# Chunked attention and a gated mixture of experts on one core: row scatters and first gathers paced by the blocks, and another order at the start

## The chip, the core and the metric

The kernel runs on one core of a Trainium2 chip. The metric is device time in microseconds (us): the median of three timed executions. A separate execution was taken with the hardware profiler; its page and its trace are what the sections below quote. Engines are named as the profile names them: PE is TensorE (PEld its weight loads), DVE VectorE, ACT ScalarE, POOL GpSimd, SP SyncE, which issues most loads.

## The reference, cut to what matters

Attention over chunks of 32 queries, each seeing 8 memory rows and a band of keys (16 to the left, 8 to the right of its chunk), feeds a mixture of 8 experts. Each token goes to one expert: a fresh argmax where a local gate is below one half, otherwise the expert of the token before it.

```python
# attention: batch 4, heads 8, seq 768, head_dim 64, n_mem 8; chunk, left, right = 32, 16, 8
for c in range(nc):
    k_full = concat([mem_k, k[:, :, l_start:r_end]]);  v_full = concat([mem_v, v[:, :, l_start:r_end]])
    scores = q_c @ k_full.T / sqrt(D)
    a = exp(scores - max);  a = a / (sum(a) + 1e-9)
    out[:, :, c_start:c_end] = a @ v_full
# bridge: (B, H, S, D) -> (B, S, H*D): x has 3072 tokens of 512

# experts: E = 8, F = 1024; w1 is (8, 512, 1024), w2 is (8, 1024, 512), all float32
logits = x @ w_gate;  local_gate = sigmoid(x @ w_local)
for b in range(B):
    prev_e = -1
    for s in range(S):
        fresh_e = argmax(logits[b, s])
        e = fresh_e if (s == 0 or local_gate[b, s] < 0.5) else prev_e
        prev_e = e
        p = softmax(logits[b, s])
        out[b, s] = p[e] * (relu(x[b, s] @ w1[e]) @ w2[e])
```

## The kernel before

The work is cut into 32 blocks of 96 tokens (NB = 32; 8 blocks a batch, NQB = 8; a half batch is HALF = 4 blocks). For each block the kernel computes transposed scores, exponentials and values, turns the block's output for the gate, and after each half batch computes logits, picks, ranks and a destination row for every token. Each block's 96 rows of x (512 values, a probability and a token number) are then scattered by an indirect DMA from the POOL queue into x_dram, where the rows of one expert stand together. Tiles of 128 rows are later gathered from there and run through one expert. The matmuls and transposes keep the program's order.

A block's work, two instructions per head in scores and one in values:

```python
def scores(qt, kt, qb):                      # 16 small matmuls with tile_position, 3 exponentials on ACT
    ...
def values(pt, vt, n, x):
    for u in range(2):
        o_ps = ops.tile([QB, HP, VW], F32, name="o_ps", tag=f"o_ps{u}")
        for a in range(HP):
            nc.tensor.matmul(o_ps[:, a], lhsT=pt[:, u, a], rhs=vt[:, 2 * a + u], start=True, stop=True)
        rinv = rinvs[:, n, u]
        nc.vector.reciprocal(rinv, o_ps[:, :, DH:VW])
        nc.vector.tensor_tensor(x[...][:, u], o_ps[:, :, 0:DH], rinv.to_broadcast([QB, HP, DH]), op=ALU.mult)

def turned(x, xt):                           # four transposes into xt_ps, then a copy on ACT
    ...
    nc.scalar.copy(xt, xt_ps)
```

The scatters of a half batch, four at once, at the end of its routing:

```python
def route_rows(r, b, half, x):
    ...
    row = sm.tile([QB, HALF], I32, name="row", bufs=2)
    nc.vector.tensor_reduce(row, r_ps, axis=AX.X, op=ALU.max)
    ...
    for n in range(HALF):
        ins = nc.gpsimd.indirect_dma_start(
            out=x_dram[:, :], out_offset=bass.IndirectOffsetOnAxis(ap=row[:, n:n + 1], axis=0),
            in_=x[0:QB, j + n].bitcast(I32), in_offset=None).ins
        ...
        scatters[b].append(ins)
```

When each step of routing runs: half batch g is routed from n = 4 g + 6 on; `first` runs ahead of a block's values, `after` behind them.

```python
for g in range(NB // HALF):
    b, half = divmod(g, 2)
    n = HALF * g + HALF + 2
    plan_at(first, n, half_logits, g)                      # lt_ps
    ...                                                    # turned logits, picks, experts, ranks: n .. n + 3
    plan_at(after, n + (4 if g in (2 * FORE - 1, 2 * B - 2, 2 * B - 1) else 5), rows, b, half)
...
n = NQB * FORE + HALF + 2                                  # 22
plan_at(after, n, plan_begun)                              # tiles of the first two batches
plan_at(after, n + 1, planned)                             # from here weights of the first two tiles
plan_at(after, n + 2, early_gathered)                      # all five early gathers
plan_at(after, NB - 3, first_turned)                       # needs the first of them
for n in range(NB - 8, NB):
    plan_at(after, n, some_pieces, 1)                      # a sixteenth of two tiles' weights each
```

The main loop and the loads ahead of it (LOADS = 4 buffers, PAIR = 2):

```python
qks = {n: load_qk(n, nc.scalar) for n in range(2)}
vts = {n: load_v(n) for n in range(LOADS - 2)}
...
begun = {n: begin(n) for n in range(PAIR)}                 # load_qk(n + 2), then scores(n)
nc.sync.dma_start(wg[:, :, 0:E], w_gate.rearrange("(k p) e -> p k e", p=P))
nc.sync.dma_start(wg[:, :, E:E + 1], w_local.rearrange("(k p) e -> p k e", p=P))
for n in range(NB):
    b, j = divmod(n, NQB)
    if n % PAIR == 0:
        for f in first.pop(n, ()):
            f()
        for m in range(n + PAIR, min(n + 2 * PAIR, NB)):
            begun[m] = begin(m)
    ...
    values(begun.pop(n), vts.pop(n), n, xs[b][0:QB, j])
    if n + LOADS - 2 < NB:
        vts[n + LOADS - 2] = load_v(n + LOADS - 2)
    if n > 0:
        turn(n - 1)
    for f in after.pop(n, ()):
        f()
```

Behind the loop come the experts' tiles: weights of one expert (4 MB a tile) into three buffers, two products, and an indirect DMA of the result rows into the output. The last routing steps (half batches 6 and 7 scatter there) stand between the matmuls of the first two tiles. The indices of the result rows are made on POOL:

```python
to = hp.tile([P, 1], I32, name="to", bufs=4)
nc.gpsimd.tensor_tensor(to, xs[:, D + 1:XW].bitcast(I32), past, op=ALU.add)
```

Of the kernel before, what the change touches and what calls it, by code (L numbers as in the profile page):

```python
# [9 lines left out]
I32 = mybir.dt.int32  # L10
ACT = mybir.ActivationFunctionType
ALU = mybir.AluOpType
# [3 lines left out]
P = 128  # L16
B, H, S, DH, NMEM = 4, 8, 768, 64, 8
CHUNK, LEFT, RIGHT = 32, 16, 8
E, F = 8, 1024
D = H * DH  # L20
DK, FK = D // P, F // P
HP = H // 2
# [5 lines left out]
QB = 96  # L28
BAND = P - NMEM
NQB = S // QB  # L30
HALF = NQB // 2
HQ = HALF * QB
NB = B * NQB
# [8 lines left out]
FORE = 2  # L42
EARLY = 5
BRANCH = SURE - 4
RING = 4
LOADS = 4
PLAN = 3 * E + 5
PAIR = 2
# [181 lines left out]
def everything(ctx, tc, q, k, v, w_gate, w_local, w1, w2, x_dram, out, ident, back):  # L230
# [4 lines left out]
    nc = tc.nc  # L235
# [29 lines left out]
    def load_v(n):  # L265
        vt = ld.tile([P, H, VW], F32, name="vt")
        nc.sync.dma_start(vt, v[n])
        return vt
# [1 line left out]

    qks = {n: load_qk(n, nc.scalar) for n in range(2)}
    qks.update({n: load_qk(n) for n in range(2, LOADS - 2)})
    vts = {n: load_v(n) for n in range(LOADS - 2)}
    table = once.tile([1, 1], F32, name="table")
    nc.scalar.activation(table, zeros[0:1, 0:1], ACT.Exp)

# [1 line left out]
    wg = once.tile([P, DK, QUARTER], F32, name="wg")  # L278
# [26 lines left out]
    for name, qb in kinds:  # L305
        lo = QB * qb - LEFT - band_start(qb) + NMEM
        hi = QB * qb + CHUNK + RIGHT - band_start(qb) + NMEM
        m = masks[name] = once.tile([P, NG], F32, name=f"mask_{name}")
# [42 lines left out]
# [4 lines that stand above are left out]
                nc.tensor.matmul(o_ps[:, a], lhsT=pt[:, u, a], rhs=vt[:, 2 * a + u], start=True, stop=True)  # L355
            rinv = rinvs[:, n, u]
            nc.vector.reciprocal(rinv, o_ps[:, :, DH:VW])
            nc.vector.tensor_tensor(  # L358
                x[:, 0:D].rearrange("p (a u d) -> p u a d", u=2, d=DH)[:, u], o_ps[:, :, 0:DH],
                rinv.to_broadcast([QB, HP, DH]), op=ALU.mult)  # L360

    def turned(x, xt):
        xt_ps = xps.tile([P, DK, QB], F32, name="xt_ps", tag="xps")
# [26 lines left out]


    scatters = {b: [] for b in range(B)}

    def begin_route():
        return {n: sm.tile([QB, NQB, w], F32, name=n, bufs=2) for n, w in (("lt", E + 1), ("ex", E))}
# [56 lines left out]
    def route_rows(r, b, half, x):  # L452

        j = HALF * half
        rank, tot, ex = r["rank"], r["tot"], r["ex"][:, j:j + HALF]
        r_ps = xps.tile([QB, HALF, E], F32, name="r_ps", tag="xps")
        for n in range(HALF):
            nc.tensor.transpose(r_ps[:, n], rank[:, QB * (j + n):QB * (j + n) + QB], identity=ident[:E, :E])
        row = sm.tile([QB, HALF], I32, name="row", bufs=2)
        nc.vector.tensor_reduce(row, r_ps, axis=AX.X, op=ALU.max)  # L460
        nc.vector.scalar_tensor_tensor(ex, r_ps, 0.0, ex, ALU.is_gt, ALU.mult)
        prob = sm.tile([QB, HALF, 1], F32, name="prob")
        nc.vector.tensor_reduce(prob, ex, axis=AX.X, op=ALU.add)
        nc.vector.tensor_tensor(x[0:QB, j:j + HALF, D:D + 1], prob, tot, op=ALU.mult)
        for n in range(HALF):
            ins = nc.gpsimd.indirect_dma_start(  # L466
                out=x_dram[:, :], out_offset=bass.IndirectOffsetOnAxis(ap=row[:, n:n + 1], axis=0),
                in_=x[0:QB, j + n].bitcast(I32), in_offset=None).ins

            tc.declare_no_dep(ins, group="scatters", query=mybir.DependencyQuery.ANY_SYNC, reason="rows are unique")  # L470
            tc.add_to_no_dep_group("scatters", ins)
            scatters[b].append(ins)

# [120 lines left out]

    SP = mybir.EngineType.SP

    def gathered(tiles, i, after, xs=None):
        _, rows, _ = tiles  # L600
        if xs is None:
            xs = gx.tile([P, XW], F32, name="xs")
        ins = nc.gpsimd.indirect_dma_start(
            out=xs.bitcast(I32), out_offset=None, in_=x_dram[:, :],
            in_offset=bass.IndirectOffsetOnAxis(ap=rows[:, i:i + 1], axis=0)).ins
        for a in after:
            for s in scatters[a]:
                tc.add_manual_dep(ins, s.name, mybir.DependencyInfo(
                    mybir.DependencyClass.Sync, mybir.DependencyReason.DATA), reason="rows written")
        tc.add_to_no_dep_group("scatters", ins)  # L610
        return xs

# [36 lines left out]
    def begin(n):  # L649
        ahead = n + LOADS - 2  # L650
        if ahead < NB:
            qks[ahead] = load_qk(ahead)
        return scores(*qks.pop(n), n % NQB)

    xs, xts, lts, routes = {}, {}, {}, {}
# [8 lines left out]
        b, half = divmod(g, 2)  # L664
        logits_turned(lts.pop(g), routes[b]["lt"][:, HALF * half:HALF * half + HALF])

    def rows(b, half):
        route_rows(routes[b], b, half, xs[b])


    first, after = {}, {}

    def plan_at(at, step, f, *args):
        at.setdefault(step, []).append(lambda: f(*args))
# [4 lines that stand above are left out]
        plan_at(first, n, half_logits, g)  # L679
        plan_at(after, n, half_turned, g)  # L680
        plan_at(after, n + 1, lambda b=b, half=half: route_picks(routes[b], half))
        plan_at(after, n + 2, lambda b=b, half=half: route_experts(routes[b], half))
        plan_at(after, n + 3, lambda b=b, half=half: route_ranks(routes[b], b, half))
        plan_at(after, n + 3, lambda b=b, half=half: route_places(routes[b], half))

        plan_at(after, n + (4 if g in (2 * FORE - 1, 2 * B - 2, 2 * B - 1) else 5), rows, b, half)

    early = {}

# [8 lines left out]
        early["w"], pieces = zip(*(weights_begun(early["tiles"], i, wa) for i in range(2)))  # L698
        early["pieces"] = [p for ps in pieces for p in ps]

    def early_gathered():
        early["xs"] = [gathered(early["tiles"], i, range(FORE)) for i in range(EARLY)]

    def rows_turned(tiles, i, xs, ps=None, xt=None):
        _, _, past = tiles
# [21 lines left out]
    n = NQB * FORE + HALF + 2  # L727
    plan_at(after, n, plan_begun)
    plan_at(after, n + 1, planned)
    plan_at(after, n + 2, early_gathered)  # L730
    plan_at(after, NB - 3, first_turned)
    for n in range(NB - 8, NB):
        plan_at(after, n, some_pieces, 1)

    begun = {n: begin(n) for n in range(PAIR)}
    nc.sync.dma_start(wg[:, :, 0:E], w_gate.rearrange("(k p) e -> p k e", p=P))
    nc.sync.dma_start(wg[:, :, E:E + 1], w_local.rearrange("(k p) e -> p k e", p=P))
    for n in range(NB):
        b, j = divmod(n, NQB)
        if n % PAIR == 0:  # L740
            for f in first.pop(n, ()):
                f()
            for m in range(n + PAIR, min(n + 2 * PAIR, NB)):
                begun[m] = begin(m)
        if j == 0:
            xs[b] = xp.tile([P, NQB, XW], F32, name="x")
            nc.gpsimd.tensor_copy(xs[b][0:QB, :, D + 1:XW].bitcast(I32), token[:, n:n + NQB])
            routes[b] = begin_route()
        if j % HALF == 0:
            xts[n // HALF] = sm.tile([P, DK, HALF, QB], F32, name="xt", bufs=2)  # L750
        values(begun.pop(n), vts.pop(n), n, xs[b][0:QB, j])
        if n + LOADS - 2 < NB:
            vts[n + LOADS - 2] = load_v(n + LOADS - 2)
        if n > 0:
            turn(n - 1)
        for f in after.pop(n, ()):
            f()
# [136 lines left out]
    for i in range(SURE):  # L894
        if i + 2 < EARLY:
            tile_w.append(weights(early["tiles"], i + 2, pools[(i + 2) % 3]))
        if i == 2:
# [3 lines left out]
            for _ in range(2):  # L901
                flat = xp.tile([P, NQB, XW], F32, name="x").rearrange("p n w -> p (n w)")
                at = 0
# [32 lines left out]
        if i + 1 < SURE:  # L936
            tiles, at_i = (early["tiles"], i + 1) if i + 1 < EARLY else (late, i + 1 - EARLY)
# [53 lines left out]
```

## Time and profile before

| | |
|---|---|
| timed, median of 3 | 498.27 us (497.16 to 498.86) |
| profiled execution | 525.75 us, span 524.0 us, mean granted clock 0.959 |
| PE busy | 493.1 us, 94% of the span |
| DVE, ACT, POOL busy | 108.8, 111.5, 98.8 us |
| moved by DMA | 146.08 MB, mean 279 GB/s |
| row scatters into x_dram | 32, 29.7 us of POOL, 927 ns each |
| first gathers | 5, 7.1 us from issue to landing |
| first lt_ps matmul | at 26.48 us |
| first expert matmul | at 137.83 us |

The page gives the busy time of each engine, then the span in 40 equal slices with the busy share in tenths, the granted clock of TensorE and the DMA share; its groups give the cost of each kind of instruction. The trace behind it answers for any stretch of time: busy time by engine, or the instructions in order with the idle time before each in brackets and what ended it.

### The profile page before, as it was taken

The page shows a single profiled execution, that of the slowest core. Times are in us where ns is not written, and L with a number is a line of the kernel's source. Part 1 is how long each engine was busy: PE and PEld are TensorE (multiplying, and loading weights), DVE is VectorE, ACT ScalarE, POOL GpSimd, SP SyncE. Part 2 cuts the span into 40 slices and gives each one's busy share as a digit, 9 for nine tenths or more (in the row PEclk, how much of TensorE's full clock was granted, in tenths as well). Part 3 has the DMA queues.
Part 4 walks back from the last instruction along what each step waited for, and adds up shares of the span by engine and source line. Part 5 has one row for each costly group of instructions (what it writes and reads, how often), then busy time and mean ns, then how long its engine had stood idle before and what let it go on. Part 6 is the DMA issues. An engine that isn't in the chain of part 4 may idle for free. (4 is left out here: it accounts for less than half of the span.)

```text
span 524.0 us, 10237 instructions
## 1 busy us (share of the span) xinstructions
PE 493.1 (94%) x3982; PEld 376.5 (72%) x3982; DVE 108.8 (21%) x437; ACT 111.5 (21%) x235; POOL 98.8 (19%) x151
## 2 busy tenths in 40 slices
PE   6998977888999999999999999999999999999993
PEld 4987865777867877777677777777767777859671
DVE  2565545643534700000100000000000000000000
ACT  4565443432211111011111111101111111101110
POOL 3002112332306212211011111111100220022201
PEclk8999778976999999999999999999999999999997
DMA  8988668699999998999899999888229999952011
GB/s 271 295 266 256 190 178 250 197 350 332 377 400 314 374 379 305 353 357 328 312 349 325 318 334 328 321 323 322 115 57 379 408 329 411 410 190 48 29 43 31
DMA packets 49381, 146.08 MB, mean 279 GB/s; under 512 B 7258, under 2 KB 11358, under 8 KB 49312
## 3 DMA queue, kind: packets, MB, share of 16 engines
q1 hardware_dynamic: 42240, 123.38, 66.2%
q0 software_dynamic: 6784, 21.30, 11.3%
q8 instruction: 38, 0.62, 0.5%
q10 hardware_dynamic: 288, 0.52, 0.3%
q14 instruction: 31, 0.25, 0.2%
HBM read 132.57 MB, written 13.00 MB: 278 GB/s over the span
## 5 line engine op out<-in xcount | busy, mean ns | idle before, releaser
L644 PE MATMUL y_ps<-w_sb,ht 128*128 128x512 f32 x224 | 98.5, 593 | 0.0
L644 PEld LDWEIGHTS h_ps<-held_xt,w_sb 128*128 128x128 f32 x704 | 80.5, 192 | 6.6 <-issue 4.9
L644 PE MATMUL h_ps<-held_xt,w_sb 128*128 128x128 f32 x704 | 81.4, 275 | 0.9 <-ACTq _compat.py:109 0.9
L644 PEld LDWEIGHTS y_ps<-w_sb,ht 128*128 128x128 f32 x224 | 41.5, 190 | 46.9 <-issue 46.2
L799 POOL DMA_INDIRECT out_dram<-y,to x24 | 24.2, 1009 | 241.9 <-ACT y L798 178.8
L644 PE MATMUL o_ps<-vt,pt 128*96 128x65 f32 x512 | 55.6, 263 | 8.2 <-DVE x L358 2.7
L644 PEld LDWEIGHTS o_ps<-vt,pt 128*96 128x96 f32 x512 | 51.4, 178 | 12.9 <-remote 2.9
L783 PEld LDWEIGHTS h_ps<-gxt,w_sb 128*128 128x128 f32 x448 | 51.2, 192 | 2.9 <-issue 2.9
L783 PE MATMUL h_ps<-gxt,w_sb 128*128 128x128 f32 x448 | 51.7, 275 | 0.0
L786 ACT ACTIVATE ht<-h_ps 128x512 f32<-128x512 f32 x42 | 25.1, 597 | 121.2 <-PE h_ps L644 76.7
L794 PE MATMUL y_ps<-w_sb,ht 128*128 128x512 f32 x112 | 49.4, 592 | 0.0
L466 POOL DMA_INDIRECT x_dram<-x,row x32 | 29.7, 927 | 93.0 <-DVE tot L448 60.6
L644 PEld LDWEIGHTS s_ps<-qt,kt 64*64 64x64 f32 x1024 | 28.7, 160 | 15.5 <-issue 11.5
L644 PE MATMUL s_ps<-qt,kt 64*64 64x96 f32 x1024 | 32.7, 283 | 6.8 <-DMA kt<-in_k_dram 3.5
L794 PEld LDWEIGHTS y_ps<-w_sb,ht 128*128 128x128 f32 x112 | 20.7, 190 | 23.0 <-issue 22.7
L711 DVE COPY held_xt<-g_ps 128x512 f32<-128x512 f32 x12 | 8.3, 689 | 137.5 <-PE g_ps L644 123.0
L644 PEld LDWEIGHTS h_ps<-x,w_sb 128*128 128x128 f32 x192 | 31.2, 190 | 1.2 <-issue 1.2
L644 PE MATMUL h_ps<-x,w_sb 128*128 128x192 f32 x192 | 31.9, 327 | 0.0
L348 ACT ACTIVATE pt<-s_ps,mask_mid 128x256 f32<-128x256 f32 x72 | 28.2, 478 | 12.3 <-PE s_ps L644 11.6
L711 DVE COPY gxt<-g_ps 128x512 f32<-128x512 f32 x10 | 6.9, 687 | 95.1 <-PE g_ps L708 52.7
L358 DVE TENSOR_TENSOR x<-o_ps,rinvs 96x256 f32<-96x256 f32 x64 | 26.2, 417 | 1.2
L798 ACT ACTIVATE y<-y_ps,x 128x512 f32<-128x512 f32 x12 | 8.2, 687 | 83.1 <-PE y_ps L644 76.4
(208 smaller groups left out, 379.3 us busy)
## 6 DMA issues: line engine op xcount, KB each, us to landing
w_sb<-in_w_dram SPq DMA_DIRECT2D x192, 512.0 KB
vt<-in_v_dram SPq DMA_DIRECT2D x32, 260.0 KB
kt<-in_k_dram SPq DMA_DIRECT2D x30, 256.0 KB
qt<-in_q_dram SPq DMA_DIRECT2D x32, 192.0 KB
kt<-in_k_dram ACTq DMA_DIRECT2D x2, 256.0 KB
x_dram<-x,row POOLq DMA_INDIRECT x32, 6.5
out_dram<-y,to POOLq DMA_INDIRECT x24, 7.5
x<-x_dram,rows_late POOLq DMA_INDIRECT x11
```

Of the source, the lines that this page charges most:

```text
L348: nc.scalar.activation(pt[:, :, :, c], st[:, :, :, c], ACT.Exp, bias=m[:, g:g + 1], scale=SCALE)
L358: nc.vector.tensor_tensor(x[:, 0:D].rearrange("p (a u d) -> p u a d", u=2, d=DH)[:, u], o_ps[:, :, 0:DH], rinv.to_broadcast([QB, HP, DH]), ...
L466: ins = nc.gpsimd.indirect_dma_start(out=x_dram[:, :], out_offset=bass.IndirectOffsetOnAxis(ap=row[:, n:n + 1], axis=0), in_=x[0:QB, j + n ...
L644: return lambda *a, **k: tc.keep_in_program_order(f(*a, **k))
L711: nc.vector.tensor_copy(xt[:, :, 0:P], g_ps)
L783: nc.tensor.matmul(h_ps[:, m], lhsT=w1_sb[:, kk, P * (g + m):P * (g + m) + P], rhs=xt[:, kk, 0:rows], start=(kk == 0), stop=(kk == DK - 1))
L786: nc.scalar.activation(ht[:, g:g + many], h_ps, ACT.Relu)
L794: nc.tensor.matmul(y_ps, lhsT=ht[:, m, 0:P], rhs=w2_sb[:, m], start=(m == 0), stop=(m == FK - 1))
L798: nc.scalar.activation(y, y_ps, ACT.Copy, scale=xs[:, D:D + 1])
L799: return apart(nc.gpsimd.indirect_dma_start(out=out, out_offset=bass.IndirectOffsetOnAxis(ap=to, axis=0), in_=y, in_offset=None, bounds_ch ...
```

## The change

Three things are moved; no arithmetic is changed, and the number of instructions on each engine stays the same but for a few waits.

- The row scatters of half batches 0, 1, 2, 4 and 5 go out one with each block: the first when the rows are known, the others behind the last VectorE multiply of the following blocks. Half batches 3, 6 and 7 still send their four at once. The five early gathers also go out one with each block, from block 24 on.
- At the start the values of block 0 come ahead of the scores of blocks 2 and 3, and block 1's v is loaded behind the q and k of blocks 2 and 3.
- The gate's weights are loaded behind the values of block 2 instead of ahead of the loop.

It is meant to keep the pipeline of TensorE, VectorE and ScalarE going while rows are scattered, and to give TensorE work while the first loads come in.

```diff
@@ -270,7 +270,7 @@
 
     qks = {n: load_qk(n, nc.scalar) for n in range(2)}
     qks.update({n: load_qk(n) for n in range(2, LOADS - 2)})
-    vts = {n: load_v(n) for n in range(LOADS - 2)}
+    vts = {0: load_v(0)}
     table = once.tile([1, 1], F32, name="table")
     nc.scalar.activation(table, zeros[0:1, 0:1], ACT.Exp)
 
@@ -355,9 +355,9 @@
                 nc.tensor.matmul(o_ps[:, a], lhsT=pt[:, u, a], rhs=vt[:, 2 * a + u], start=True, stop=True)
             rinv = rinvs[:, n, u]
             nc.vector.reciprocal(rinv, o_ps[:, :, DH:VW])
-            nc.vector.tensor_tensor(
+            paced[0] = nc.vector.tensor_tensor(
                 x[:, 0:D].rearrange("p (a u d) -> p u a d", u=2, d=DH)[:, u], o_ps[:, :, 0:DH],
-                rinv.to_broadcast([QB, HP, DH]), op=ALU.mult)
+                rinv.to_broadcast([QB, HP, DH]), op=ALU.mult).ins
 
     def turned(x, xt):
         xt_ps = xps.tile([P, DK, QB], F32, name="xt_ps", tag="xps")
@@ -390,6 +390,12 @@
 
 
     scatters = {b: [] for b in range(B)}
+
+    paced = [None]
+
+    def behind(ins, name):
+        tc.add_manual_dep(ins, name, mybir.DependencyInfo(
+            mybir.DependencyClass.Sync, mybir.DependencyReason.DATA), reason="rows written, or one a block")
 
     def begin_route():
         return {n: sm.tile([QB, NQB, w], F32, name=n, bufs=2) for n, w in (("lt", E + 1), ("ex", E))}
@@ -462,14 +468,18 @@
         prob = sm.tile([QB, HALF, 1], F32, name="prob")
         nc.vector.tensor_reduce(prob, ex, axis=AX.X, op=ALU.add)
         nc.vector.tensor_tensor(x[0:QB, j:j + HALF, D:D + 1], prob, tot, op=ALU.mult)
-        for n in range(HALF):
-            ins = nc.gpsimd.indirect_dma_start(
-                out=x_dram[:, :], out_offset=bass.IndirectOffsetOnAxis(ap=row[:, n:n + 1], axis=0),
-                in_=x[0:QB, j + n].bitcast(I32), in_offset=None).ins
-
-            tc.declare_no_dep(ins, group="scatters", query=mybir.DependencyQuery.ANY_SYNC, reason="rows are unique")
-            tc.add_to_no_dep_group("scatters", ins)
-            scatters[b].append(ins)
+        r["row"] = row
+
+    def scatter(r, b, half, n):
+        j = HALF * half + n
+        ins = nc.gpsimd.indirect_dma_start(
+            out=x_dram[:, :], out_offset=bass.IndirectOffsetOnAxis(ap=r["row"][:, n:n + 1], axis=0),
+            in_=xs[b][0:QB, j].bitcast(I32), in_offset=None).ins
+
+        tc.declare_no_dep(ins, group="scatters", query=mybir.DependencyQuery.ANY_SYNC, reason="rows are unique")
+        tc.add_to_no_dep_group("scatters", ins)
+        scatters[b].append(ins)
+        return ins
 
 
 
@@ -596,7 +606,7 @@
 
     SP = mybir.EngineType.SP
 
-    def gathered(tiles, i, after, xs=None):
+    def gathered(tiles, i, after, xs=None, then=None):
         _, rows, _ = tiles
         if xs is None:
             xs = gx.tile([P, XW], F32, name="xs")
@@ -605,8 +615,9 @@
             in_offset=bass.IndirectOffsetOnAxis(ap=rows[:, i:i + 1], axis=0)).ins
         for a in after:
             for s in scatters[a]:
-                tc.add_manual_dep(ins, s.name, mybir.DependencyInfo(
-                    mybir.DependencyClass.Sync, mybir.DependencyReason.DATA), reason="rows written")
+                behind(ins, s.name)
+        if then is not None:
+            behind(ins, then.name)
         tc.add_to_no_dep_group("scatters", ins)
         return xs
 
@@ -664,8 +675,14 @@
         b, half = divmod(g, 2)
         logits_turned(lts.pop(g), routes[b]["lt"][:, HALF * half:HALF * half + HALF])
 
-    def rows(b, half):
+    def rows(b, half, count):
+
         route_rows(routes[b], b, half, xs[b])
+        for n in range(count):
+            scatter(routes[b], b, half, n)
+
+    def moved(b, half, n):
+        behind(scatter(routes[b], b, half, n), paced[0].name)
 
 
     first, after = {}, {}
@@ -683,7 +700,13 @@
         plan_at(after, n + 3, lambda b=b, half=half: route_ranks(routes[b], b, half))
         plan_at(after, n + 3, lambda b=b, half=half: route_places(routes[b], half))
 
-        plan_at(after, n + (4 if g in (2 * FORE - 1, 2 * B - 2, 2 * B - 1) else 5), rows, b, half)
+        if g in (2 * FORE - 1, 2 * B - 2, 2 * B - 1):
+            plan_at(after, n + 4, rows, b, half, HALF)
+        else:
+            at = min(n + 5, NB - 2)
+            plan_at(after, at, rows, b, half, 1)
+            for j in range(1, HALF):
+                plan_at(after, min(at + j, NB - 1), moved, b, half, j)
 
     early = {}
 
@@ -698,8 +721,8 @@
         early["w"], pieces = zip(*(weights_begun(early["tiles"], i, wa) for i in range(2)))
         early["pieces"] = [p for ps in pieces for p in ps]
 
-    def early_gathered():
-        early["xs"] = [gathered(early["tiles"], i, range(FORE)) for i in range(EARLY)]
+    def early_gathered(i):
+        early.setdefault("xs", []).append(gathered(early["tiles"], i, range(FORE), then=paced[0]))
 
     def rows_turned(tiles, i, xs, ps=None, xt=None):
         _, _, past = tiles
@@ -727,21 +750,26 @@
     n = NQB * FORE + HALF + 2
     plan_at(after, n, plan_begun)
     plan_at(after, n + 1, planned)
-    plan_at(after, n + 2, early_gathered)
+    for i in range(EARLY):
+        plan_at(after, n + 2 + i, early_gathered, i)
     plan_at(after, NB - 3, first_turned)
     for n in range(NB - 8, NB):
         plan_at(after, n, some_pieces, 1)
 
     begun = {n: begin(n) for n in range(PAIR)}
-    nc.sync.dma_start(wg[:, :, 0:E], w_gate.rearrange("(k p) e -> p k e", p=P))
-    nc.sync.dma_start(wg[:, :, E:E + 1], w_local.rearrange("(k p) e -> p k e", p=P))
+    vts[1] = load_v(1)
+
+    def pair_begun(n):
+        for m in range(n + PAIR, min(n + 2 * PAIR, NB)):
+            begun[m] = begin(m)
+
     for n in range(NB):
         b, j = divmod(n, NQB)
         if n % PAIR == 0:
             for f in first.pop(n, ()):
                 f()
-            for m in range(n + PAIR, min(n + 2 * PAIR, NB)):
-                begun[m] = begin(m)
+            if n > 0:
+                pair_begun(n)
         if j == 0:
             xs[b] = xp.tile([P, NQB, XW], F32, name="x")
             nc.gpsimd.tensor_copy(xs[b][0:QB, :, D + 1:XW].bitcast(I32), token[:, n:n + NQB])
@@ -749,6 +777,11 @@
         if j % HALF == 0:
             xts[n // HALF] = sm.tile([P, DK, HALF, QB], F32, name="xt", bufs=2)
         values(begun.pop(n), vts.pop(n), n, xs[b][0:QB, j])
+        if n == 0:
+            pair_begun(n)
+        if n == PAIR:
+            nc.sync.dma_start(wg[:, :, 0:E], w_gate.rearrange("(k p) e -> p k e", p=P))
+            nc.sync.dma_start(wg[:, :, E:E + 1], w_local.rearrange("(k p) e -> p k e", p=P))
         if n + LOADS - 2 < NB:
             vts[n + LOADS - 2] = load_v(n + LOADS - 2)
         if n > 0:
```

## The prediction

> **What bounds the kernel now.** I read the page's slices first, then the busy time by stretches, then the order of time inside the worst stretches. The slices split the span:
>
> ```profile
> PE   6998977888999999999999999999999999999993
> ...
> PEclk8999778976999999999999999999999999999997
> DMA  8988668699999998999899999888229999952011
> ```
>
> A slice is 13.1 us. From the eleventh on (about 132 us) TensorE is full and at full clock: this is the expert stage. In the ten before it, the attention and routing, TensorE has holes and its clock falls. To size both I cut the span at the logits matmuls (lt_ps), which come once in four blocks:
>
> ```profile
> 16.48:26.48 10.00, 10.00 (x209) 9.53 (x209) 4.80 (x17) 6.51 (x16) 0.00 (x0) 1.00 0.88 284
> 26.48:38.12 11.64, 11.61 (x226) 10.44 (x225) 6.49 (x30) 7.58 (x19) 0.00 (x0) 1.00 0.85 261
> 38.12:53.83 15.71, 12.98 (x229) 11.19 (x229) 9.01 (x39) 8.10 (x20) 3.75 (x4) 0.91 0.84 261
> 53.83:72.18 18.35, 15.02 (x229) 12.86 (x229) 9.50 (x42) 7.32 (x18) 3.69 (x5) 0.78 0.67 203
> 72.18:89.12 16.94, 13.52 (x230) 11.42 (x229) 8.50 (x36) 8.09 (x20) 3.86 (x5) 0.90 0.72 219
> 89.12:106.40 17.28, 14.65 (x234) 12.41 (x234) 11.71 (x63) 7.10 (x18) 5.62 (x6) 0.92 0.62 192
> 106.40:132.08 25.68, 21.56 (x232) 18.64 (x232) 10.37 (x42) 7.98 (x20) 6.58 (x7) 0.68 0.98 341
> ...
> 140.00:518.00 378.00, 374.60 (x2161) 274.36 (x2159) 37.67 (x124) 50.99 (x86) 69.07 (x93) 1.00 0.78 288
> ```
>
> Columns: the stretch, its length, then busy time and count of PE, PEld, DVE, ACT and POOL, the granted clock, DMA share and GB/s. Four blocks without a scatter (26.48 to 38.12) take 11.64 us with TensorE full. Every later four blocks hold row scatters (POOL busy) and take 15.7 to 25.7 us for the same 229 or so matmuls. The experts are 374.6 busy of 378: nothing in this change can shorten them. What a scatter burst does shows in the order of time:
>
> ```profile
> 46.10 1.00 POOL L466 DMA_INDIRECT x_dram<-x,row  x1 [40.41 <-DVE tot L448]
> ...
> 47.40 0.92 POOL L466 DMA_INDIRECT x_dram<-x,row  x1 [0.30 <-issue]
> ...
> 47.50 0.50 PE L644 MATMUL xt_ps<-ident,x 96*128 96x96 f32 x4
> ...
> 48.18 0.18 DVE L357 RECIPROCAL rinvs<-o_ps 96x4 f32<-96x4 f32 x1 [1.67 <-PE xt_ps L644]
> ...
> 48.63 0.92 POOL L466 DMA_INDIRECT x_dram<-x,row  x1 [0.30 <-issue]
> ...
> 49.85 0.92 POOL L466 DMA_INDIRECT x_dram<-x,row  x1 [0.30 <-issue]
> ...
> 51.77 0.48 ACT L366 COPY xt<-xt_ps 128x384 f32<-128x384 f32 x1 [3.80 <-PE o_ps L644]
> ```
>
> The four transposes xt_ps end at 48.00 and ScalarE has been free since 47.96, but its copy starts at 51.77, 1.0 us after the last of four scatters has been issued (50.77). VectorE too starts late. Nothing that they wait for by name is missing; everything halts together while POOL emits row scatters, then TensorE's clock is halved.
>
> **The number that decides the size.** The profiled execution took 525.75 us, the timed ones 498.27: 27.5 us less. The experts are full in the profile, so nearly all of it must come out of the stage with the holes. Its excess over 11.64 us for four blocks is 4.07 + 6.71 + 5.30 + 5.64 + 14.04 = 35.8 us. So only about 35.8 - 27.5 = 8.3 us of excess can be left when no profile is taken. I read most of the halts as an effect of recording 96 rows for each scatter. That is an inference; no run here shows it yet. The pacing is worth a part of 8 us, not of 36.
>
> **What the Trainium skill says.** "TensorE: Matmul & The Clock Gate", section "What's actually happening": the array falls to half clock after an idle window of about 3.4 us and comes back after a busy one. The trace agrees: in 10.00 to 15.00 us, after a hole of 3.0 us in the start, the granted clock averages 0.66. "SBUF — State Buffer", section "Who interferes with whom": only VectorE and GpSimd can block each other, TensorE and ScalarE wait on no one. The trace shows ScalarE late by 3.8 us, so a port lock is not the cause. "Perfetto Trace Analysis", section on the SWDGE instruction: its slice is the making of descriptors, not the transfer. It agrees: 0.92 us slices, 6.5 us from issue to landing on the page.
>
> **The change, part by part.**
>
> *Start: values of block 0 ahead of scores 2 and 3, block 1's v behind their loads, gate weights later.* Now: scores 0 and 1 end at 6.85; scores 2 and 3 wait for kt until 9.83 and, the clock having fallen at about 10, take 2.79 us instead of 1.55; values 0 and 1 follow at 12.55; scores 4 and 5 start at 16.48. Loads ahead of them, from the page's sizes (qt 192 KB, kt 256, vt 260): four qt and kt pairs and two vt, 2312 KB = 2.37 MB by 9.83. At 321 GB/s (stretch 4.00 to 16.48, DMA share 1.00) that is 7.4 us, so the stream counts from about 2.4. After: one vt less, 0.27 MB / 321 = 0.8 us, so scores 2 and 3 start at 9.0. Values 0 (1.5 us) fill the hole at about 7.0, so I expect full clock: scores 2 and 3 end at 10.55, values 1 at 12.1, transposes at 12.4. Scores 4 and 5 need 2052 + 260 + 896 KB = 3.29 MB: 2.4 + 10.2 = 12.7. **That is 3.8 us before 16.48.** The next pair: TensorE would be ready at 12.7 + 5.0 (a pair, 16.48 to 21.48) = 17.7; the data, with three more vt and two qt, kt pairs, is 5.0 MB, 2.4 + 15.6 = 18.0, plus 0.6 for the gate's small pieces, which now stand here (from 8.50 to 9.50 DMA moved 175 GB/s where the us before moved 409: 0.57 us lost). So scores 6 and 7 start at 18.6 instead of 21.48: 2.9 us are left. Later the load stream has slack (share 0.85 to 0.88 from 16 to 38 us), so I carry 2.9, call it **3.0**.
>
> *Paced scatters.* Number of instructions unchanged: 32 scatters. Five of eight half batches (0, 1, 2, 4, 5) send one row scatter behind each block's last VectorE multiply; half batch 3 still sends four at once, because the first gathers need it, and 6 and 7 lie under the experts. Half batch 5 is cut off by the end of attention: one scatter at block 30 and three at 31, three of which POOL takes only after the result indices, which wait for the end of attention (11.5 us today). In the timed runs the five stretches keep 8.3 of 35.8 us, a factor of 0.23. The first three, whose bursts are all paced, hold 16.1, so 3.7 us timed. A single scatter still costs its 0.92 us of POOL and perhaps one short halt, so I count under half: **1.5 us**.
>
> *Paced gathers.* Five, now after blocks 22+2 to 22+6, not all at block 24. Only the first is needed before the experts (block 29). The same traffic, spread; the last stretch (106 to 132) has DMA share 0.98 with two tiles' weights. I count **0**: what is not DMA-bound there may gain, what is DMA-bound can't.
>
> Sum: 498.3 - 3.0 - 1.5 = **493.8**.
>
> **Rivals.**
> 1. *The halts are real without a profile and pacing removes them.* For it: 36 us of excess are in plain view. Against: the timed runs lack 27.5 of them. If all of the 8.3 went, with the start: 498.3 - 11.3 = 487.
> 2. *A halt comes with each scatter and is only spread.* Then the sum of halts stays, though holes under the clock's window may keep the clock up. The start alone remains: 495.3; with new holes in four times as many blocks, 499.
> 3. *DMA takes the place of the saved time.* From block 24 the loads of the last blocks, two tiles' weights (8.4 MB) and the gathers share the engines; 0.98 share, 341 GB/s. If the experts' start waits for weights, what was saved after the plan (block 23) is lost, though a saving before block 23 brings the weights forward too. Then 495 to 497.
>
> **Range and chances.** Start 2 to 4 us, pacing -2 to +6, DMA taking back 0 to 2. The eight-in-ten range is 488 to 498.5. Two per cent is 10 us, which needs rival 1 almost whole: 0.09. Slower by 10 us has no mechanism here: 0.02.
>
> **What would show it.** In the profile after: values of block 0 at about 7 us, scores 4 and 5 before 13.5, scores 6 and 7 before 19.5, no half clock at 10; if scores 4 still start after 15, the start is wrong. Stretches of four blocks between logits matmuls: nearer 12 to 14 us than 15 to 18 if pacing keeps the clock up; unchanged if halts only spread. Half batch 3's burst should still show its halt. Even a much shorter profiled span (by 15 us, say) with a timed gain of 4 to 5 would be as I expect, since the profile exaggerates the halts. The prediction is wrong if the timed gain passes 10 us (the halts were real, the 0.23 factor false), or if there is none (the start's gain was taken back by the loads).

## The result, and the profile after

The changed kernel takes 491.68 us (median of four runs, 490.64 to 492.67) against 497.72 us (four runs, 496.92 to 498.86) before: a ratio of 0.9877, interval 0.9847 to 0.9907. That is 6.0 us, where 4.5 us had been predicted. The total was near, but one step on the way to it was false, and the nearness is in part luck.

The slices of the profiled execution of the changed kernel (span 490.1 us, 12.3 us a slice) answer to those of before:

```profile
PE   8999999899999999999999999999999999999993
...
PEclk9999999999999999999999999999999999999998
...
DMA  8978999999999999988989898894179999921111
```

The holes of the first ten slices and the low clock beside them are nearly gone. The busy time by stretches, cut at the logits matmuls as before (length, then busy time and count of PE, PEld, DVE, ACT and POOL, granted clock, DMA share, GB/s):

```profile
23.09:34.73 11.64, 11.60 (x225) 10.44 (x225) 6.49 (x30) 7.59 (x19) 0.00 (x0) 1.00 0.82 264
34.73:46.71 11.98, 11.88 (x229) 10.70 (x229) 9.02 (x39) 7.65 (x20) 1.92 (x2) 1.00 0.83 261
46.71:58.63 11.92, 11.88 (x229) 10.70 (x229) 8.93 (x40) 7.53 (x20) 4.13 (x4) 1.00 0.94 292
58.63:70.61 11.98, 11.88 (x229) 10.71 (x229) 9.01 (x39) 7.65 (x20) 3.89 (x5) 1.00 0.99 316
70.61:83.95 13.34, 12.95 (x235) 11.34 (x235) 11.93 (x65) 7.53 (x19) 6.42 (x7) 1.00 0.98 310
83.95:98.94 14.99, 13.57 (x233) 12.05 (x233) 10.38 (x40) 8.07 (x20) 3.85 (x4) 0.92 1.01 364
98.94:108.87 9.93, 9.64 (x93) 8.27 (x92) 6.10 (x33) 2.12 (x5) 2.95 (x3) 0.95 1.01 404
```

Four blocks with scatters now take 11.92 to 11.98 us, with TensorE full. Even the fifth stretch, where half batch 3 still sends four at once, holds 12.95 us of PE in 13.34. It is in truth five in a row (75.39 to 80.28 us, 1.2 us apart), since the last scatter of half batch 2 falls on the same block 22. Only the sixth has a hole: TensorE waits 1.42 us for vt at 95.57 and runs at half clock from about 96.5 to 100. What follows the last logits matmul took 381 to 383 us in every recording compared here, so all differences lie ahead of it.

The profiled spans differ by 33.9 us (524.0 to 490.1), the timed runs by 6.0. The prediction read that as an effect of recording. The first experiment shows that recording alone does not bring the halts.

### The profile page after: what moved, and what is told of

Same layout as the page of the kernel before. It is cut to its first block, busy times and chain, and to the rows that moved or that the text cites. A ratio compares the mean times of both kernels' runs of the same rounds, so it can differ in the third digit from the quotient of the medians.

```text
span 490.1 us, 10242 instructions
## 1 busy us (share of the span) xinstructions
PE 476.3 (97%) x3982; PEld 364.2 (74%) x3982; DVE 109.0 (22%) x437; ACT 111.5 (23%) x235; POOL 101.1 (21%) x151
## 5 line engine op out<-in xcount | busy, mean ns | idle before, releaser
L655 PE MATMUL o_ps<-vt,pt 128*96 128x65 f32 x512 | 50.2, 251 | 1.7 <-DMA vt<-in_v_dram 1.4
L655 PEld LDWEIGHTS o_ps<-vt,pt 128*96 128x96 f32 x512 | 46.9, 166 | 5.4 <-issue 1.6
L475 POOL DMA_INDIRECT x_dram<-x,row x32 | 31.3, 978 | 63.3 <-DVE tot L454 40.8
L655 PEld LDWEIGHTS s_ps<-qt,kt 64*64 64x64 f32 x1024 | 23.0, 138 | 6.9 <-DMA qt<-in_q_dram 3.1
L734 DVE COPY gxt<-g_ps 128x512 f32<-128x512 f32 x10 | 6.9, 689 | 95.3 <-PE g_ps L731 52.8
L655 PE MATMUL s_ps<-qt,kt 64*64 64x96 f32 x1024 | 26.3, 254 | 0.9 <-DMA kt<-in_k_dram 0.9
L831 ACT ACTIVATE y<-y_ps,xs 128x512 f32<-128x512 f32 x12 | 8.3, 688 | 81.9 <-PE y_ps L827 48.3
```

The lines of the kernel that those rows point to most:

```text
L475: ins = nc.gpsimd.indirect_dma_start(out=x_dram[:, :], out_offset=bass.IndirectOffsetOnAxis(ap=r["row"][:, n:n + 1], axis=0), in_=xs[b][0: ...
L655: return lambda *a, **k: tc.keep_in_program_order(f(*a, **k))
L734: nc.vector.tensor_copy(xt[:, :, 0:P], g_ps)
L831: nc.scalar.activation(y, y_ps, ACT.Copy, scale=xs[:, D:D + 1])
```

## The experiments

All runs on one chip share the runs of the kernel before, taken beside them. Chips are called A to D in order of use; each served for one group of runs only. Ratios leave out runs more than 1.5% above the fastest of their kernel, so they differ a little from the quotient of two medians; microseconds of a gain are the ratio times the median before, unless medians are named. The stretches are four blocks each, between logits matmuls, from one recording of each kernel.

| run | chip | ratio to before | interval | first logits matmul, us | second to fourth stretch, us | fifth | sixth and seventh |
|---|---|---|---|---|---|---|---|
| before again | A | 0.9986 | 0.9959 to 1.0012 | 25.71 | 11.98, 11.92, 11.97 | 13.28 | 14.68, 16.62 |
| start only | A | 0.9948 | 0.9924 to 0.9972 | 23.31 | 11.98, 11.92, 12.13 | 13.27 | 13.65, 12.70 |
| pacing only | A | 0.9865 | 0.9816 to 0.9914 | 28.92 | 11.98, 11.92, 11.98 | 13.35 | 12.56, 9.46 |
| gathers at once | A | 0.9874 | 0.9835 to 0.9913 | 23.23 | 11.98, 11.91, 11.98 | 13.49 | 12.56, 13.58 |
| early bursts | B | 0.9831 | 0.9785 to 0.9876 | 24.32 | 16.59, 18.46, 17.77 | 18.45 | 13.86, 9.64 |
| gathers late | B | 0.9921 | 0.9899 to 0.9944 | 23.71 | 15.84, 18.99, 17.35 | 18.02 | 17.48, 10.23 |
| weights late | B | 0.9966 | 0.9942 to 0.9989 | 23.22 | 16.58, 18.69, 17.93 | 18.51 | 23.19, 10.14 |
| v ahead | B | 0.9590 | 0.9547 to 0.9632 | 23.44 | 12.53, 12.52, 12.61 | 20.97 | 14.65, 10.00 |
| changed again | C | 0.9538 | 0.9497 to 0.9579 | 25.65 | 11.98, 12.63, 12.64 | 21.13 | 14.94, 9.46 |
| all paced | C | 0.9480 | 0.9422 to 0.9538 | 24.77 | 11.98, 12.58, 12.65 | 14.56 | 14.08, 10.00 |
| plain writes | C | 0.9548 | 0.9494 to 0.9602 | 26.21 | 11.98, 12.52, 12.74 | 21.80 | 14.34, 9.46 |
| plain writes by GpSimd | D | 0.9953 | 0.9919 to 0.9988 | 22.71 | 11.99, 11.91, 19.06 | 15.03 | 12.56, 9.46 |

**The same kernel before takes 499.6 us on chip A (43 runs), 499.0 on D (20), 523.8 on B (43) and 524.6 on C (11).** The ranges do not touch: 504.9 us is the slowest on A and D, 520.3 the fastest on B and C. The timed 498 us of the comparison and the profile of 525.75 us with its halts fit these two kinds of chip. So the profile of before most likely showed a chip of the other kind than the one on which the kernel was timed. The chips of these two are not on record, nor that of the changed kernel's comparison, whose times and stretches are those of A. As no chip was used twice, it also isn't shown that a chip stays of its kind.

### Before, unchanged

No edit. 

> The kernel before, unchanged, recorded and timed again. If the halts under scatter bursts come from recording that form of program, a new profile again lies 20 us or more above the timed 497.7, with stretches of four blocks of 15 us and more. If they belonged to one recorded execution alone, the new profile lies within 3 us of the timed runs and the stretches with scatters take 12 to 13 us.

Its profiled execution took 500.58 us, amid its 20 timed ones (496.15 to 503.01, median 499.25): a recording need not hold any halt, nor take longer. By these numbers the expectation's second case came true, but its reason, one odd execution, doesn't fit the halts that every recording with bursts on chips B and C shows. Stretches of this recording (columns as above):

```profile
37.34:49.32 11.98, 11.88 (x228) 10.70 (x228) 9.02 (x39) 7.65 (x20) 3.08 (x4) 1.00 0.83 251
49.32:61.24 11.92, 11.88 (x229) 10.70 (x229) 8.95 (x40) 7.54 (x20) 3.72 (x5) 1.00 1.03 301
...
86.49:101.17 14.68, 12.53 (x233) 11.09 (x233) 9.88 (x40) 8.07 (x20) 8.54 (x9) 1.00 0.98 358
101.17:117.79 16.62, 13.93 (x93) 12.85 (x93) 6.79 (x33) 2.04 (x5) 3.84 (x8) 0.69 1.03 367
```

These are the same bursts of four scatters and they cost nothing: in the first of these stretches PE is 11.88 us busy of 11.98. One such burst in the order of time:

```profile
46.63 0.92 POOL L466 DMA_INDIRECT x_dram<-x,row  x1 [0.30 <-issue]
...
46.73 0.50 PE L644 MATMUL xt_ps<-ident,x 96*128 96x96 f32 x4
...
47.26 0.48 ACT L366 COPY xt<-xt_ps 128x384 f32<-128x384 f32 x1
...
47.85 0.92 POOL L466 DMA_INDIRECT x_dram<-x,row  x1 [0.30 <-issue]
```

ScalarE copies xt_ps 0.03 us after the transposes end, in the middle of the burst. In the profile before, the copy of such a burst started 3.8 us after its transposes. What the recording on chip A does show is a loss at the end of the attention. Its waits of TensorE for v:

```profile
98.72 1.54 PE L644 MATMUL o_ps<-vt,pt 128*96 128x65 f32 x16 [2.03 <-DMA vt<-in_v_dram]
104.72 2.63 PE L644 MATMUL o_ps<-vt,pt 128*96 128x65 f32 x16 [2.69 <-DMA vt<-in_v_dram]
```

Behind the second one the array runs at half clock until about 115 us, which is the 0.69 of the last stretch. The DMA share there is 0.98 to 1.03, so the DMA engines had hardly a gap in which v could have come sooner: the gathers, the scatters and two tiles' weights move beside it.

### Start only

Of the diff, only the start: v of block 1 behind the first scores' loads, values of block 0 ahead of scores 2 and 3, gate weights behind block 2's values. Scatters and gathers stay as before. 

> Only the new order at the start (values of block 0 first, block 1's v and the gate's weights later); scatters and gathers still in bursts. Start theory: 3.4 us of the 6.0 (the first logits matmul came 3.39 us earlier in the two profiles), so 494.3. If the start is the whole gain: 491.7. If what the start saves is lost again in the later stages: 497.

The ratio 0.9948 of 499.62 us is 2.6 us (1.4 to 3.8). The first logits matmul comes 2.40 us sooner than in the recording of before on this chip. The waits for v at the end are 1.00, 2.12 and 1.19 us.

### Pacing only

The changed kernel with the old start. 

> Only the paced scatters and gathers; the start as before. If pacing is worth the rest: 497.7 - 2.6 = 495.1. If pacing is worth nothing: 497.7. If the halts of a burst are real in timed runs and the start worth little: 492 or less.

It gains 1.35%, 6.7 us (4.3 to 9.2), more than the 2.6 expected as the rest, and as much as the whole change. By size this is the third of the expected cases, but the halts that it names are not in the recordings of this chip. In the recording the last two stretches take 22.02 us instead of 31.30, with no wait for v. The start fell late in this execution (28.92 us, TensorE waited 1.89 us for kt), so the loads were ahead of TensorE by more than in the others. How much of the quiet end is due to that was not separated.

### Gathers at once

```diff
     for i in range(EARLY):
-        plan_at(after, n + 2 + i, early_gathered, i)
+        plan_at(after, n + 2, early_gathered, i)
```

> The changed kernel, but its five early gathers all behind block 24; the scatters stay paced. My prediction counted 0 for the pacing of the gathers: 491.7. If five gathers at once hold up the loads of the last blocks and the weights: 493 to 494.

0.9874, against 0.9877 for the whole change: the pacing of the gathers isn't worth anything that can be measured on such a chip. In the recording TensorE waits 0.15 and 2.09 us for v, in the changed kernel 1.42.

These four recordings and that of the changed kernel give the loss at the end in one sum. Take the 22.02 us of pacing only as the floor of the last two stretches, and add the waits for v and the clock not granted, (1 - clock) times the length:

| recording | last two, us | over 22.02 | waits for v | clock not granted |
|---|---|---|---|---|
| before again | 31.30 | 9.28 | 4.72 | 0.31 x 16.62 = 5.15 |
| start only | 26.35 | 4.33 | 4.31 | 0 |
| gathers at once | 26.14 | 4.12 | 2.24 | 0.13 x 13.58 = 1.77 |
| changed | 24.92 | 2.90 | 1.42 | 0.08 x 14.99 + 0.05 x 9.93 = 1.70 |

The two causes make up the loss to within 0.6 us. The recordings are single executions, though. That of start only was the fastest of its 22, and its end is no worse than that of gathers at once, whose scatters are paced. So what the loss consists of is shown. That pacing the scatters is what shortens it rests on the timed runs alone: 6.3 us (4.3 to 8.2) for gathers at once against 2.6 (1.4 to 3.8) for the start, whose intervals just part.

### Early bursts

Half batches 0, 1 and 2 send four scatters at once again, the rest as in the changed kernel.

```diff
-        if g in (2 * FORE - 1, 2 * B - 2, 2 * B - 1):
-            plan_at(after, n + 4, rows, b, half, HALF)
+        if g in (2 * FORE - 1, 2 * B - 2, 2 * B - 1) or g < 2 * FORE:
+            plan_at(after, n + (4 if g in (2 * FORE - 1, 2 * B - 2, 2 * B - 1) else 5), rows, b, half, HALF)
```

> The changed kernel with the scatters of half batches 0, 1 and 2 in bursts of four again; half batches 4 and 5 and the gathers stay paced. My prediction's step (a burst halts the engines, 1.5 us timed): 1 to 1.5 us slower than the changed kernel, that is 0.991 of the kernel before. New theory (only the DMA load of blocks 24 to 31 counts): no loss, 0.987 to 0.988; stretches 2 to 4 stay at 11.9 to 12.0 us.

This ran on chip B, and neither expectation held: the ratio is 0.983. Two stretches with bursts:

```profile
52.62:71.08 18.46, 15.04 (x230) 12.86 (x229) 8.98 (x39) 7.81 (x19) 3.73 (x5) 0.78 0.70 202
71.08:88.85 17.77, 14.91 (x229) 12.72 (x228) 9.04 (x38) 7.70 (x19) 3.83 (x5) 0.79 0.71 210
```

Here are the halts of the profile before, and they are in the timed runs as well: the profiled execution took 514.79 us, the timed median is 514.85. The same two stretches, paced, in the run v ahead on the same chip:

```profile
47.61:60.13 12.52, 12.07 (x229) 10.76 (x229) 8.85 (x40) 7.53 (x20) 4.13 (x4) 1.00 0.90 291
60.13:72.74 12.61, 12.10 (x229) 10.78 (x229) 8.93 (x39) 7.66 (x20) 4.32 (x5) 1.00 0.94 295
```

A burst costs 4.1 to 5.9 us for each half batch.

### Gathers late, and weights late

Both keep the bursts of before and have the new start alone. The first moves gathers 2 to 4 behind block 31, the second starts the weights at block 26:

```diff
+    plan_at(after, NB - 1, others_gathered)        # gathers late: three of five
-    for n in range(NB - 8, NB):                    # weights late
+    for n in range(NB - 6, NB):
```

> Only the new start, all scatters in bursts; of the early gathers two go out behind block 24 and three behind block 31. New theory (gathers compete with v loads of the last blocks): waits for v fall from 4.3 us to 1.5 or less, ratio 0.988 instead of 0.995 for the start alone. If the bursts of scatters are what costs: no gain over the start alone, 0.995.

> Only the new start, bursts as before; the pieces of the first two tiles' weights start two blocks later (blocks 26 to 31 one each, the rest behind them). New theory: fewer waits for v, by half or more, so 0.990; but the weights of tile 0 may then come late and take it back: 0.995. If DMA is not the cause: 0.995 with the same waits.

In both recordings the waits for v are gone; with late gathers the kernel gains 0.8%, with late weights 0.3%. As the start is in both and wasn't run alone on chip B, and as the halts there delay TensorE and so hide the loads, neither says what the same edit gives on chip A. What they do show is that gathers in a row halt as scatters do. In weights late five gathers go out from 103.32 to 109.35. Transposes end at 106.88, and ScalarE, free since 105.89, copies them only behind the last gather:

```profile
108.40 0.95 POOL L603 DMA_INDIRECT xs<-x_dram,rows_early  x1 [0.30 <-issue]
...
110.58 0.48 ACT L366 COPY xt<-xt_ps 128x384 f32<-128x384 f32 x1 [4.69 <-remote]
```

The sixth stretch is 23.19 us with five gathers and 17.48 with two; the weights' start differs too.

### v ahead

The changed kernel, with v loaded three blocks ahead instead of two from block 20.

```diff
+        if n == 20:
+            vts[22] = load_v(22)
+        far = n + LOADS - (1 if n >= 20 else 2)
-        if n + LOADS - 2 < NB:
-            vts[n + LOADS - 2] = load_v(n + LOADS - 2)
+        if far < NB:
+            vts[far] = load_v(far)
```

> The changed kernel, and from block 20 on v is loaded three blocks ahead instead of two. New theory: the last wait for v (1.42 us in the profile of the changed kernel) and the half clock behind it go: 1 to 2.5 us faster than the changed kernel, 0.983 to 0.986 of the kernel before. If something else sets the end of the attention: 0.988.

The main finding is what this run has in common with the change. On the same chip as early bursts its ratio is 0.959 instead of 0.983: pacing the first three half batches, with v loaded earlier, is worth 12.3 us there by the medians (514.85 and 502.51). The second to fourth stretch fall from 52.8 to 37.7 us. The fifth takes 2.5 back: it has five scatters in a row where early bursts has four. Loading v earlier was not timed apart: the changed kernel itself ran on C, not on B, and its 0.954 against 0.959 here gives no sign of a gain; the expected 0.983 to 0.988 had no halts in view. The one burst left, that of half batch 3, still halts; in the order of time:

```profile
79.34 0.50 PE L655 MATMUL xt_ps<-ident,x 96*128 96x96 f32 x4
...
81.23 0.92 POOL L475 DMA_INDIRECT x_dram<-x,row  x1 [0.30 <-issue]
81.85 0.48 ACT L366 COPY xt<-xt_ps 128x384 f32<-128x384 f32 x1 [4.38 <-PE s_ps_early L655]
```

The copy's input is complete at 79.84, and nothing on ScalarE stands ahead of it, but it starts at 81.85.

### Changed again, and all paced

The changed kernel without an edit on chip C, and beside it a version that paces the last early burst too (half batch 3 at blocks 22 to 25, gathers behind blocks 26 to 30, the first gathered rows turned at block 30, and v ahead as above).

```diff
-        if g in (2 * FORE - 1, 2 * B - 2, 2 * B - 1):
+        if g in (2 * B - 2, 2 * B - 1):
...
-            at = min(n + 5, NB - 2)
+            at = min(n + (4 if g == 2 * FORE - 1 else 5), NB - 2)
...
-        plan_at(after, n + 2 + i, early_gathered, i)
-    plan_at(after, NB - 3, first_turned)
+        plan_at(after, n + 4 + i, early_gathered, i)
+    plan_at(after, NB - 2, first_turned)
```

> The changed kernel, unchanged, beside the others. On a chip where the kernel before takes about 498: 0.987 to 0.988. On a chip where it takes about 524 (bursts halt the engines there): single scatters hardly halt them, so about 0.962, stretches 2 to 4 near 12.5 us, and only the burst of half batch 3 keeps its halt (about 21 us in stretch 5).

> The changed kernel with v three blocks ahead from block 20 on, half batch 3 paced as well (blocks 22 to 25), the early gathers behind blocks 26 to 30 and the first tile turned at block 30. Where bursts halt the engines: the last burst goes, stretch 5 falls from 21 to about 14 us, 5 to 7 us faster than the changed kernel. Where they don't: 1 to 2 us faster than it through v, or the same if the later gathers hold up tile 0 or 1.

On this chip the change is worth 23 us by the medians: 501.27 against 524.64. The fifth stretch, with the burst left in, and then without it in all paced:

```profile
74.54:95.67 21.13, 17.96 (x234) 15.72 (x234) 12.36 (x66) 7.21 (x19) 6.95 (x7) 0.77 0.84 258
```

```profile
73.61:88.17 14.56, 13.27 (x235) 11.61 (x235) 11.73 (x64) 7.25 (x20) 5.04 (x5) 1.00 0.88 269
```

6.6 us less, and the clock stays up. One gather has left this stretch too (changed again, at 92.26), but the halt lies ahead of it, at the five scatters from 79.46 to 84.35. All paced has the lowest time seen on such a chip: a median of 496.32 us, 5 us under the changed kernel beside it. Four of its six runs took 495.2 to 496.7 us, two took 501.8 and 502.4, and the intervals of the two ratios overlap. On a chip like A it wasn't run.

### Plain writes, from two queues

The changed kernel with four plain writes (96 rows of x each, to a spare array) added behind the routing of half batches 0, 1 and 2, first from the SyncE queue, then from GpSimd. Its scatters stay paced.

```diff
+        if g < 3:
+            for n in range(HALF):
+                at = HQ * g + QB * n
+                nc.sync.dma_start(aside[at:at + QB], xs[b][0:QB, HALF * half + n].bitcast(I32))    # or nc.gpsimd
```

> The changed kernel, and in addition the rows of half batches 0, 1 and 2 are copied in bursts of four plain writes from the SP queue to a spare array in DRAM, at the blocks where the bursts of scatters stood. If the halts come from writing 4 x 193 KB to DRAM at once: stretches 2 to 4 grow to 16 us and more on a chip that shows halts. If they come from the indirect DMA of the POOL queue: stretches stay at 12 to 13 us, and only the added 2.4 MB and the SP queue's waits may cost 1 to 3 us.

> The changed kernel with bursts of four plain writes added behind the gates of half batches 0, 1 and 2, as in the run of plain writes, but issued by GpSimd instead of the SyncE queue; all scatters of these half batches stay paced. Theory A: what halts the engines is a burst of DMAs whose descriptors GpSimd makes in software, whether they are indirect or not. Then, on a chip where the kernel before takes some 524 us, the second to fourth stretch of four blocks take 16 us or more each (against 12.0 to 12.7 in the changed kernel there), and the time is 510 to 516 us. Theory B: it takes the indirect form (rows by a list). Then these stretches stay at 12.0 to 13 us and the time is 500 to 504 us on such a chip. On a chip where the kernel before takes some 498 us neither halts anything: the stretches stay at 12 to 12.5 us, the time at 491 to 494 us, and the run doesn't tell the two apart.

From SyncE, on chip C, the writes go out in rows of four at 45.61, 57.61 and 71.04 us, one row in each of the second to fourth stretch. The last two of these:

```profile
49.83:62.35 12.52, 12.07 (x230) 10.78 (x229) 8.86 (x40) 8.01 (x20) 4.14 (x4) 1.00 1.02 347
62.35:75.09 12.74, 12.18 (x229) 10.84 (x229) 9.00 (x39) 7.25 (x20) 4.35 (x5) 1.00 1.04 332
```

They took 12.63 and 12.64 us without the writes. The bytes and the writes do not halt anything. From GpSimd the run fell on chip D, which doesn't halt, so it doesn't tell GpSimd's descriptors from the indirect form. Its time of 498.07 us missed the 491 to 494 expected there. Its longest stretch has another cause than a halt:

```profile
68.99 1.56 PE L657 MATMUL s_ps<-qt,kt 64*64 64x96 f32 x32 [3.01 <-DMA kt<-in_k_dram]
```

The DMA share was 1.05 in that stretch. From 40 to 72 us the loads of k took 9.1 to 12.9 us from issue to landing, in the changed kernel's recording 4.2 to 6.0. So added writes made a load late, and the array then ran at half clock (0.74 for the stretch).

## Why the prediction was right, and where its reasoning failed

**Start, 3.0 us: right when timed alone.** The order of time of the changed kernel:

```profile
7.10 1.88 PE L655 MATMUL o_ps<-vt,pt 128*96 128x65 f32 x16
...
8.91 1.55 PE L655 MATMUL s_ps<-qt,kt 64*64 64x96 f32 x64
...
12.23 0.89 PE L655 MATMUL s_ps<-qt,kt 64*64 64x96 f32 x32
...
13.38 0.89 PE L655 MATMUL s_ps<-qt,kt 64*64 64x96 f32 x32 [0.26 <-DMA kt<-in_k_dram]
...
17.73 1.55 PE L655 MATMUL s_ps<-qt,kt 64*64 64x96 f32 x64
```

Values of block 0 had been put at 7.0, scores 2 and 3 at 9.0 in 1.55 us, scores 4 and 5 at 12.7, scores 6 and 7 at 18.6; the last came 0.9 us sooner. Timed alone the start gave 2.6 us. On top of the pacing it shows no gain: 0.9865 without it, 0.9877 with it, and the intervals are too wide to say more. One part of it isn't sure to come: in the recordings of changed again, all paced and plain writes, scores 2 and 3 still took 2.84 us instead of 1.55, and the first logits matmul came at 24.8 to 26.2 us.

**The number that decides the size: false.** This is the step that failed. "I read most of the halts as an effect of recording", with the factor 0.23 that followed from it, most likely compared two chips without knowing it. There is no factor between recorded and timed runs: they agree on A (500.58 and 499.25 us) as on B (514.79 and 514.85). The chips of these runs are of two kinds, with all of the halts or none of them. The first three stretches with bursts, to which the factor gave 3.7 us of excess, hold 0.95 in the recording on A (11.98, 11.92 and 11.97, less three times 11.64), with TensorE full.

**Paced scatters, 1.5 us: too small, and for a reason that does not hold.** On A no halt was left to take away. What pacing gained there, 3.5 us if the whole change is set against the start (6.1 - 2.6) and 3.7 with the gathers at once (6.3 - 2.6), can only be looked for in the last two stretches, the second to fifth being equal within 0.3 us. The loss there is waits for v and the half clock that follows them, which the prediction left out of this term. With the old start pacing gained 6.7. So the terms were 3.0 and 1.5 where the runs gave 2.6 and 6.7, each alone, and 6.1 for both: that 4.5 came near the total is luck. On B and C rival 1 holds in full, and goes beyond its own estimate: 23 us on C, not 11.

**Paced gathers, 0: right on A** (0.9874 and 0.9877). GpSimd's order of time in the changed kernel shows that two of the five are not where the program put them:

```profile
100.24 0.96 POOL L613 DMA_INDIRECT xs<-x_dram,rows_early  x1 [7.38 <-DMA x_dram<-x,row]
...
109.59 0.97 POOL L613 DMA_INDIRECT xs<-x_dram,rows_early  x1 [5.79 <-DMA x_dram<-x,row]
```

They wait for the landing of earlier scatters, up to 7.38 us, and go out at the end of the attention or behind it. Those are scatters of half batch 4, whose rows they don't need. In the code only scatters are declared free of dependencies on x_dram, not gathers, so the program itself may ask for this wait; no run tells.

**Rival 2, halts only spread: refuted on B and C.** Single scatters leave 12.5 to 12.7 us for four blocks, 0.5 to 0.8 over the 11.98 of A, where bursts take 16 to 19.

**Rival 3, DMA in the place of what was saved: the place was right.** The end of the attention is where DMA binds, with a share of 1.0. But the loss there was part of the kernel before, 9.3 us in the recording on A, and grew smaller with the change, to 2.9. The start and the pacing timed apart sum to 9.3 us, together they give 6.1 (4.6 to 7.6). The intervals leave open whether that is a real overlap at this shared limit.

**The checks named in the prediction.** All those of the start held. Stretches of 12 to 14 us came, but on A they come with bursts too, so that check couldn't tell its theory from this one. "Half batch 3's burst should still show its halt" failed in the changed kernel's profile (13.34 us, clock 1.00) and held on B and C (21 us). And a much shorter profiled span beside a small timed gain, which was to confirm the effect of recording, came for another reason: it had been a sign as good for two chips.

## What to carry to other kernels

When a profile and the timed runs differ by several per cent, record the same kernel again beside timed runs on one chip before inferring anything from the difference. Send indirect DMAs one with each block rather than four in a row: where bursts halt the engines, three half batches of it, with v loaded earlier, were worth 12 us of 515 and the whole change 23 of 525, and elsewhere it cost nothing. Where the DMA share is 1.0 ahead of a stage that cannot wait, look at which transfers are not needed yet, and count the half clock behind a wait as part of the wait's price.

## What the runs showed of the hardware

- The same program took 499 us on two chips and 524 on two others. On the latter a row of four or five indirect DMAs from GpSimd, scatters or gathers, stops ScalarE for 2.0 to 3.8 us (its copies above), TensorE for 2.0 (v ahead, 80.37 to 82.38, with no wait named) and VectorE for 2.7 (weights late, 107.81 to 110.52). Single ones hardly stop them (12.5 to 12.7 us for four blocks), and plain writes from SyncE not at all. What in a chip, in how a program lies on it or in the time of the run makes this so is open, and so is whether the indirect form or GpSimd's descriptors do it.
- A short hole is enough for the half clock. The Trainium skill, "TensorE: Matmul & The Clock Gate", section "What's actually happening", names an idle window of about 3.4 us. The hole of 3.0 us that the prediction took for agreement is already shorter than that. In the later runs a hole of 1.42 us (changed, at 94.15 to 95.57) was followed by half clock for some 3.5 us, and one of 2.69 us (before again) by 10 us, with TensorE busy all along; the 2.12 us of start only brought none. So the half clock cost, beside the wait itself, from nothing to 1.9 times its length (0.31 x 16.62 = 5.15 us behind 2.69).
- At the start of the program the granted clock doesn't show the slow matmuls: in changed again it reads 1.00 from 7 to 13 us, while the scores of blocks 2 and 3 take 2.84 us instead of 1.55.
